# Crossbar transposes for late blocks, relu and last sums on other engines, and a gate in two 16-bit steps, in a fused attention and highway kernel

## Chip, cores and metric

One core of a Trainium2 chip. The metric is device microseconds of one execution; beside it stands one profiled execution, whose span (first to last instruction) is a little shorter than its time. Engines: TensorE (PE), VectorE (DVE), ScalarE (ACT), GpSimd (POOL) and SyncE (SP), which here only issues DMAs.

## What is computed

```python
B, H, S, D = 4, 8, 768, 64        # attention with 4 sink keys and a window of 128
scores = q @ k.T / sqrt(D)
keep   = (key < 4) | ((query - key >= 0) & (query - key < 128))
a      = softmax(where(keep, scores, -1e9))
x      = heads_joined(a @ v)      # 3072 rows x 512
Hm     = maximum(x @ w_h, 0)
T      = sigmoid(x @ w_t + b_t)
out    = T * Hm + (1 - T) * x     # float32
```

## The kernel before

The 3072 rows are 24 blocks of 128, six for each batch. A block needs its own keys and those of the block before it, besides the four sink keys. The first block of a batch has one key chunk, the others two, and from the third on the sinks are added.

For block n: `load_qk` and `load_v` (L86, L87, L94) bring q, k and v in with DMAs that GpSimd issues and that cast to 16 bits. `pe_T` transposes q and k of all heads on TensorE into PSUM, `act_T` (L204) copies them to SBUF as `qk`. `pe_S` makes the scores for two groups of heads, `act_S` (L252) the exponentials `e`, `dve_mask` (L263) masks them. `pe_A` multiplies by v, which carries a column of constants so that the row sums come out as well; `dve_rec` and `dve_x` (L294, L299) normalise to `xh`. `pe_X` and `act_X` (L318) transpose `xh` to `xT`. `pe_Mh` (L341) and `pe_Mt` (L326, L328) are the projections by w_h and w_t; `act_u` (L334) is a tanh. `dve_d` (L347), `dve_e` (L353) and `dve_o` (L359) make the output, and SP stores it (L361).

The column of constants is 2, so that `xh` is x/2, and bias and output are scaled to fit: with u the tanh, `dd` is max(h, 0) - xh, `ee` is (u + 1) times dd, and `otok` is 2 xh + ee. Each of the three is one fused VectorE instruction.

The order on all five queues is written out by hand. In pass i of the main loop stand, among others, `pe_T(i+2)`, the second mask of block i, the scores of i+1, the transpose of x of i-1, the attention sums of i, then the projections of the blocks m whose `m + lag(m)` is i (i-1 here), then the first mask of i+1. The output of a block follows one pass after its projections. A sink product (`pe_sink`, `act_sink`) stands ahead of the projections in two passes of six. `XBAR` names blocks whose x would be transposed by a DMA of SP (`sp_X`); it is empty here. GpSimd's queue holds all the loads, up to eight blocks ahead (`AHEAD`), and a few small steps for the sinks (L213, L130).

PSUM tiles `tp`, `xtp`, `sk`, `hps` and `tps` share a pool of two buffers, `sps` has two of its own, `av` one. SBUF tiles `u`, `dd` and `ee` have three each, `otok` four, `qk` five, `xh` and `xT` seven.

Of the kernel before, what the change touches and what calls it, by code (L numbers as in the profile page):

```python
# [8 lines left out]
FP16 = mybir.dt.float16  # L9
FP32 = mybir.dt.float32  # L10
AF = mybir.ActivationFunctionType
ALU = mybir.AluOpType
# [8 lines left out]
def kernel(  # L21
# [18 lines left out]
    nc = tc.nc  # L40
    P = 128

    B, H, S, D = q.shape
# [5 lines left out]
    NT, DM = out.shape  # L49
# [4 lines left out]
    NB = NT // P  # L54
    NHP = H // 2
# [4 lines left out]

    const = ctx.enter_context(tc.tile_pool(name="const", bufs=1))
    sd_pool = ctx.enter_context(tc.tile_pool(name="p_sd", bufs=AHEAD))
    qkT_pool = ctx.enter_context(tc.tile_pool(name="p_qkT", bufs=5))
    e_pool = ctx.enter_context(tc.tile_pool(name="p_e", bufs=5))
    r_pool = ctx.enter_context(tc.tile_pool(name="p_r", bufs=3))
    x_pool = ctx.enter_context(tc.tile_pool(name="p_x", bufs=7))
    td_pool = ctx.enter_context(tc.tile_pool(name="p_td", bufs=3))
# [5 lines left out]
    NV = AHEAD + 4  # L73
    NS4 = H * NSINK
    KW = NHP * P + 32
    XBAR = ()
    LATE = 0
    v_ring = [const.tile([P, VW], FP16, tag=f"v{i}", name=f"v{i}") for i in range(NV)]
    qk_sd = {}
# [14 lines left out]
        nc.gpsimd.dma_start(out=vt[:, :, 0:D], in_=v[b, :, rows, :].transpose([1, 0, 2]))  # L94

    def init_v(vt):
        nc.vector.memset(vt[:, 0:H * 65].rearrange("p (h e) -> p h e", e=65)[:, :, D:D + 1], 2.0)
        nc.vector.memset(vt[:, H * 65:VW], 0.0)

    warm = const.tile([P, DM], FP16, tag="warm")  # L100
# [5 lines left out]
    bm = const.tile([P, H], FP16, tag="bm", name="bm")  # L106
    wh_sb = const.tile([P, NOC, DM], FP16, tag="wh")
    wt_sb = const.tile([P, NOC, DM], FP16, tag="wt")
    bt32 = const.tile([1, DM], FP32, tag="bt32")
    bt16 = const.tile([P, DM], FP16, tag="bt16")  # L110
# [26 lines left out]
    with tc.manual_schedule(engines={ENG.Pool}):  # L137
        load_qk(0)
        nc.gpsimd.affine_select(
            out=ident, in_=ident, compare_op=ALU.is_equal, fill=0.0,  # L140
# [4 lines left out]
            out=mask[:, 1, :], in_=mask[:, 1, :], compare_op=ALU.is_ge, fill=0.0,  # L145
            base=0, pattern=[[1, P]], channel_multiplier=-1)
        nc.gpsimd.affine_select(
            out=mask[:, 0, :], in_=mask[:, 0, :], compare_op=ALU.is_ge, fill=0.0,
# [6 lines left out]
            out=bm, in_=bm, compare_op=ALU.is_ge, fill=0.0,  # L155
# [10 lines left out]
    def more_constants():  # L166
        nc.vector.memset(bt16, 0.0)
        nc.vector.memset(ones_row, 0.0)
        nc.vector.memset(ones_row[0:1, :], 1.0)
        for i in range(2):  # L170
            nc.vector.memset(ks_bd[i], 0.0)
            nc.vector.memset(vs_bd[i], 0.0)
            nc.vector.memset(es_t[i], 0.0)
        nc.vector.tensor_copy(out=mask0, in_=mask[:, 1, :])
        nc.vector.memset(mask0[0:NSINK, :], 1.0)
        nc.vector.tensor_copy(out=mask1, in_=mask)
        nc.vector.memset(mask1[0:NSINK, 0, :], 1.0)
        nc.vector.tensor_scalar_mul(bt16[0:1, :], bt32, 0.5)

    def sink_ones():  # L180
        for i in range(2):
            nc.vector.tensor_scalar_mul(vs_bd[i][0:NS4, :, D:D + 1],
                                        bm[0:NS4, :].unsqueeze(2), 2.0)

    def warm_up(n):
        w = m_ps.tile([P, DM], FP32, tag="m", name="wps")
# [1 line left out]
            nc.tensor.matmul(w, lhsT=warm[:, 0:P], rhs=warm, start=True, stop=True)  # L188

    qkT, tp_of, s_of, e_of, av_of, rec_of = {}, {}, {}, {}, {}, {}  # L190
    xtp_of, xh_of, xT_of, t_of, u_of, h_of, dd_of, ee_of, sk_of = {}, {}, {}, {}, {}, {}, {}, {}, {}

    def pe_T(n):
        qsd, ksd = qk_sd.pop(n)
# [7 lines left out]
    def act_T(n):  # L202
        qk = qkT_pool.tile([P, 2 * NHP, P], FP16, tag="qk", name="qk")
        nc.scalar.copy(out=qk, in_=tp_of.pop(n))  # L204
        qkT[n] = (qk[:, 0:NHP, :], qk[:, NHP:2 * NHP, :])

    def pool_sink(b):
# [123 lines left out]

    def act_u(n):
        u = td_pool.tile([P, DM], FP16, tag="u", name="u")
        nc.scalar.activation(out=u, in_=t_of.pop(n), func=AF.Tanh)  # L334
        u_of[n] = u

    def pe_Mh(n):
        xT = xT_of[n]
        hps = m_ps.tile([P, DM], FP32, tag="m", name="hps")
        for kc in range(NOC):  # L340
            nc.tensor.matmul(hps, lhsT=xT[:, kc, :], rhs=wh_sb[:, kc, :],  # L341
                             start=(kc == 0), stop=(kc == NOC - 1))
        h_of[n] = hps

    def dve_d(n):
        dd = td_pool.tile([P, DM], FP16, tag="dd", name="dd")
        nc.vector.scalar_tensor_tensor(out=dd, in0=h_of.pop(n), scalar=0.0, in1=xh_of[n],  # L347
                                       op0=ALU.max, op1=ALU.subtract)
        dd_of[n] = dd

    def dve_e(n):
        ee = td_pool.tile([P, DM], FP16, tag="ee", name="ee")
        nc.vector.scalar_tensor_tensor(out=ee, in0=u_of.pop(n), scalar=1.0, in1=dd_of.pop(n),  # L353
                                       op0=ALU.add, op1=ALU.mult)
        ee_of[n] = ee

    def dve_o(n):
        otok = o_pool.tile([P, DM], FP32, tag="otok", name="otok")
        nc.vector.scalar_tensor_tensor(out=otok, in0=xh_of.pop(n), scalar=2.0, in1=ee_of.pop(n),  # L359
                                       op0=ALU.mult, op1=ALU.add)  # L360
        nc.sync.dma_start(out=out[n * P:(n + 1) * P, :], in_=otok)  # L361

    def on(n):
        return 0 <= n < NB
# [14 lines left out]
    with tc.manual_schedule(engines={ENG.PE, ENG.DVE, ENG.Activation, ENG.SP, ENG.Pool}):  # L379
        for i in range(-2, NB + 2):  # L380
            ms = [m for m in range(2, NB) if m + lag(m) == i]
            os_ = [m for m in range(1, NB) if m + lag(m) == i - 1]
            if i == -2:
                warm_up(8)
                more_constants()
                pe_T(0)
                act_T(0)
            elif i == -1:
                pe_S(0, 0)
                act_S(0, 0)  # L390
                pe_S(0, 1)
                act_S(0, 1)
                dve_mask(0, 0)
                dve_mask(0, 1)
                pe_T(1)
                act_T(1)
                pe_A(0)
                dve_rec(0)
                dve_x(0)
                pe_S(1, 0)  # L400
                act_S(1, 0)
                pe_S(1, 1)
                act_S(1, 1)
                dve_mask(1, 0)
                dve_mask(1, 1)
                pe_X(0)
                act_X(0)
                spare(3)
                pe_A(1)
                dve_rec(1)  # L410
                dve_x(1)
                sink_ones()
                sink_v(0, nc.vector)
            elif i == 0:
                pe_Mt(0)
                act_u(0)
                pe_X(1)
                act_X(1)
                pe_Mt(1)
                pe_Mh(0)  # L420
                dve_d(0)
                act_u(1)
                pe_T(2)
                act_T(2)
                dve_e(0)
                pe_Mh(1)
                dve_o(0)
                dve_d(1)
            elif i == 1:
                pe_S(2, 0)  # L430
                act_S(2, 0)
                dve_mask(2, 0)
                pe_S(2, 1)
                pe_T(3)
                act_T(3)
                act_S(2, 1)
                pe_sink(2)
                act_sink(2)
            else:
                if on(i + 2):  # L440
                    pe_T(i + 2)
                    act_T(i + 2)
                if on(i):
                    dve_mask(i, 1)
                for o in os_:
                    dve_e(o)
                if on(i + 1):
                    pe_S(i + 1, 0)
                    pe_S(i + 1, 1)
                if on(i - 1) and i - 1 not in XBAR and i - 1 > 1:  # L450
                    pe_X(i - 1)
                    act_X(i - 1)
                if on(i + 1):
                    act_S(i + 1, 0)
                for o in os_:
                    dve_o(o)
                if on(i):
                    pe_A(i)
                    dve_rec(i)
                    dve_x(i)  # L460
                    if i in XBAR:
                        sp_X(i)
                if has_sink(i + 1):
                    pe_sink(i + 1)
                    act_sink(i + 1)
                if on(i + 1):
                    act_S(i + 1, 1)
                for m in ms:
                    pe_Mh(m)
                    dve_d(m)  # L470
                    pe_Mt(m)
                    act_u(m)
                if on(i + 1):
                    dve_mask(i + 1, 0)
            if on(i + 2) and (i + 2) % NSC == 0:
                b = (i + 2) // NSC
                pool_sink(b)
                if b:
                    sink_v(b, nc.gpsimd)
                if b + 1 < B:  # L480
                    load_sink_v(b + 1)
            for n in {-2: range(3, AHEAD + 1), 0: [], 1: [10, 11]}.get(i, [i + 2 + AHEAD]):
                if n < NB:
                    if n > 3:
                        load_qk(n)
                    load_v(n)
# [35 lines left out]
```

## Time and profile before

| | |
|---|---|
| time, median of 2 | 129.54 us (129.47 to 129.61) |
| span of the profiled execution | 127.8 us |
| PE busy, matmul | 110.1 us (86%) |
| DVE busy | 101.8 us (80%) |
| ACT busy | 97.6 us (76%) |
| POOL busy | 74.9 us (59%), nearly all before 78 us |
| mean granted TensorE clock | 0.992 |
| 16 DMA engines | 90% or more till about 80 us, then about 20% |

Busy time of one engine is not its distance from its peak, and shares over the whole span mix the start, the passes and the end. The chain that ended last is read back from the last instruction, each step to what released it; its pieces in order of time show which dependence sets the length of a pass. Timelines of single engines list instructions with their starts, so that the distance from one start to the next can be read, which is what adds up on an engine whose neighbours overlap a little.

### The profile page before, as it was taken

The numbers are of one execution on the slowest core, as the hardware profiler recorded it, in microseconds if no ns is written. First come the engines' busy times: TensorE is split into PE (matmuls) and PEld (weight loads), VectorE is DVE, ScalarE is ACT, GpSimd is POOL, SyncE is SP. The second block draws the span as 40 slices with busy tenths as digits, with TensorE's granted clock in tenths as the row PEclk, the third lists the DMA queues.
The fourth block names the chain that finished last, engine by engine and source line by source line (L and its number), as shares of the span: only waits on it lengthen the run. The fifth ranks groups of instructions, "written<-read, shape, count | busy, mean of one in ns | idle before, by whom it ended". The sixth has DMA issues, their size and how long they took to land.

```text
span 127.8 us, 3253 instructions
## 1 busy us (share of the span) xinstructions
PE 110.1 (86%) x1315; PEld 67.9 (53%) x1315; DVE 101.8 (80%) x214; ACT 97.6 (76%) x129; POOL 74.9 (59%) x98
## 2 busy tenths in 40 slices
PE   6758989569999899999998999999989999999620
PEld 2236434447755574586555656755655666564300
DVE  6544626495999898998998998989989999899760
ACT  4066435999897998998987989989969989893310
POOL 6999939999899989999999995005000000000000
PEclk9999999999999999999999999999999999999996
DMA  0999999999999999999999999922022202210222
GB/s 1 105 126 140 165 153 157 180 181 197 160 156 204 204 180 201 163 199 200 164 199 194 208 159 205 186 95 82 8 82 82 82 5 82 82 60 28 82 82 82
DMA packets 79728, 17.00 MB, mean 133 GB/s; under 512 B 75617, under 2 KB 76641, under 8 KB 79714
## 3 DMA queue, kind: packets, MB, share of 16 engines
q0 software_dynamic: 76256, 10.51, 122.6%
q1 hardware_dynamic: 3458, 6.30, 13.3%
q8 instruction: 10, 0.16, 0.5%
q14 instruction: 4, 0.03, 0.1%
HBM read 21.01 MB, written 6.29 MB: 214 GB/s over the span
## 4 chain that ended last, share of the span: by engine, by line
PE 39%; ACT 29%; DMA 12%; POOL 9%; DVE 6%; issue 3%; POOLq 0%; ACTq 0%
PE tps L328 14%; PE hps L341 11%; ACT qk L204 10%; DMA wh_sb<-in_moe_w_h_dram 7%; ACT u L334 6%; ACT e L252 6%; ACT xT L318 5%; DMA ksd<-in_k_dram 5%; PE tps L326 4%; POOL qsd L86 3%; PE sps L244 3%; PE av L280 2%; POOL ksd L87 2%; POOL v L94 2%; PE xtp L313 2%
## 5 line engine op out<-in xcount | busy, mean ns | idle before, releaser
L252 ACT ACTIVATE e<-sps,ebias 128x1024 f16<-128x1024 f32 (+1 forms) x48 | 48.6, 1054 | 1.8 <-PE sps L244 1.8
L263 DVE TENSOR_TENSOR e<-e,mask 128x1024 f16<-128x1024 f16 (+1 forms) x48 | 29.1, 640 | 4.7 <-ACT e L252 4.6
L204 ACT COPY qk<-tp 128x1024 f16<-128x1024 f16 x24 | 24.2, 1009 | 6.4 <-PE tp L199 6.4
L341 PE MATMUL hps<-wh_sb,xT 128*128 128x512 f16 x96 | 24.8, 380 | 3.4 <-ACT xT L318 2.9
L334 ACT ACTIVATE u<-tps 128x512 f16<-128x512 f32 x24 | 14.3, 597 | 16.0 <-PE tps L328 16.0
L328 PE MATMUL tps<-wt_sb,xT 128*128 128x512 f16 x96 | 25.0, 384 | 0.1
L86 POOL DMA_DIRECT2D qsd<-in_q_dram x24 | 22.4, 932 | 3.4 <-DMA wh_sb<-in_moe_w_h_dram 2.0
L94 POOL DMA_DIRECT2D v<-in_v_dram x24 | 22.3, 929 | 0.5 <-DVE dd L347 0.3
L347 DVE SCALAR_TENSOR_TENSOR dd<-hps,xh 128x512 f16<-128x512 f32 x24 | 16.6, 691 | 7.4 <-PE hps L341 5.7
L87 POOL DMA_DIRECT2D ksd<-in_k_dram x24 | 22.1, 920 | 0.5 <-PE tps L328 0.3
L353 DVE SCALAR_TENSOR_TENSOR ee<-u,dd 128x512 f16<-128x512 f16 x24 | 16.5, 689 | 3.5 <-ACT u L334 3.2
L280 PE MATMUL av<-v,e 128*128 128x66 f16 x352 | 17.7, 197 | 0.6 <-DVE e L263 0.5
L328 PEld LDWEIGHTS <-xT 128*128 128x128 f16 x96 | 9.4, 98 | 15.0 <-issue 4.1
L299 DVE TENSOR_TENSOR xh<-av,rec 128x512 f16<-128x512 f32 x24 | 16.6, 692 | 0.8
L359 DVE SCALAR_TENSOR_TENSOR otok<-xh,ee 128x512 f32<-128x512 f16 x24 | 16.6, 692 | 0.8
L280 PEld LDWEIGHTS <-e 128*128 128x128 f16 x352 | 15.2, 100 | 2.2 <-DVE e L263 1.9
L244 PE MATMUL sps<-qk 64*128 64x128 f16 x352 | 14.6, 223 | 1.5 <-ACT qk L204 1.5
L318 ACT COPY xT<-xtp 128x512 f16<-128x512 f16 x24 | 14.4, 598 | 0.4 <-PE xtp L313 0.3
L341 PEld LDWEIGHTS <-xT 128*128 128x128 f16 x96 | 7.9, 97 | 12.0 <-ACT xT L318 5.7
L244 PEld LDWEIGHTS <-qk 64*128 64x128 f16 x352 | 10.4, 97 | 4.8 <-ACT qk L204 1.4
L199 PE MATMUL tp<-ident,ksd 128*128 128x128 f16 x96 | 9.8, 227 | 1.7 <-DMA ksd<-in_k_dram 1.6
L197 PEld LDWEIGHTS <-qsd 128*128 128x128 f16 x96 | 7.2, 100 | 6.8 <-DMA qsd<-in_q_dram 2.2
(51 smaller groups left out, 100.2 us busy)
## 6 DMA issues: line engine op xcount, KB each, us to landing
out_dram<-otok SPq DMA_DIRECT2D x24, 256.0 KB, 4.5
qsd<-in_q_dram POOLq DMA_DIRECT2D x24, 128.0 KB, 6.5
ksd<-in_k_dram POOLq DMA_DIRECT2D x24, 128.0 KB, 6.5
v<-in_v_dram POOLq DMA_DIRECT2D x24, 128.0 KB, 6.7
wt_sb<-in_moe_w_t_dram POOLq DMA_DIRECT2D x1, 512.0 KB, 7.3
wh_sb<-in_moe_w_h_dram POOLq DMA_DIRECT2D x1, 512.0 KB, 9.4
vd<-in_v_dram POOLq DMA_DIRECT2D x4, 4.0 KB, 4.9
bt<-in_moe_b_t_dram SPq DMA_DIRECT2D x1, 2.0 KB
```

The lines of the kernel that those rows point to most:

```text
L86: nc.gpsimd.dma_start(out=qsd, in_=q[b, :, rows, :].transpose([1, 0, 2]))
L87: nc.gpsimd.dma_start(out=ksd, in_=k[b, :, rows, :].transpose([1, 0, 2]))
L94: nc.gpsimd.dma_start(out=vt[:, :, 0:D], in_=v[b, :, rows, :].transpose([1, 0, 2]))
L204: nc.scalar.copy(out=qk, in_=tp_of.pop(n))
L244: nc.tensor.matmul(sps[:, hh, o:o + P], lhsT=kk[rows, hp, :], rhs=qT[rows, hp, :], start=True, stop=True)
L252: nc.scalar.activation(out=e.rearrange("p a b c d -> p a (b c d)"), in_=sps[:, :, 0:2 * np_ * P], func=AF.Exp, bias=ebias, scale=SCALE)
L263: nc.vector.tensor_tensor(out=ev, in0=ev, in1=m.unsqueeze(1).to_broadcast([P, 4, np_ * P]), op=ALU.mult)
L280: nc.tensor.matmul(av[:, g, 2 * hl + hh, 0:_AVN], lhsT=e[:, hh, hl, pc, :], rhs=vt[:, 65 * h:65 * h + _AVN], start=first, stop=False, skip ...
L318: nc.scalar.copy(out=xT, in_=xtp_of.pop(n))
L328: nc.tensor.matmul(tps, lhsT=xT[:, kc, :], rhs=wt_sb[:, kc, :], start=False, stop=(kc == NOC - 1))
L334: nc.scalar.activation(out=u, in_=t_of.pop(n), func=AF.Tanh)
L341: nc.tensor.matmul(hps, lhsT=xT[:, kc, :], rhs=wh_sb[:, kc, :], start=(kc == 0), stop=(kc == NOC - 1))
```

## The change

- q and k of blocks 12 to 23 are no longer transposed on TensorE and copied by ScalarE. `sp_T` issues two transposing DMAs from SP instead, four passes ahead of the block (in pass i for block i+4); `qk` gets eight buffers.
- x of blocks 15 to 21 is transposed by a DMA of SP (`XBAR`), and the projections of those blocks come two passes behind, not one.
- For blocks 14 to 22 (`LT`) ScalarE makes relu(h) in 16 bits (`act_r`), `dd` is a difference of two 16-bit tiles in SBUF, and the last sum runs on GpSimd.
- The column of constants becomes 1, so that `xh` is x. The gate is one step (0.5 u + 0.5, tile `tg`) and `ee` a product of two 16-bit tiles; the last sum needs no factor.

On SP the transposes stand between the output stores, in the order of the program. In pass i that is: q and k of i+4, the store of the block whose output is due, x of i. On GpSimd the sums of blocks 14 to 22 stand behind the loads of the last block. In pass 16 no projection is due, and in pass 23 there are two, of 21 and 22.

```diff
-    qkT_pool = ctx.enter_context(tc.tile_pool(name="p_qkT", bufs=5))
+    qkT_pool = ctx.enter_context(tc.tile_pool(name="p_qkT", bufs=8))
...
-    XBAR = ()
+    XBAR = range(15, 22)
+    XT = range(12, NB)
+    LT = range(14, NB - 1)
...
-        nc.vector.memset(... [:, :, D:D + 1], 2.0)
+        nc.vector.memset(... [:, :, D:D + 1], 1.0)
...
+    def sp_T(n):
+        qsd, ksd = qk_sd.pop(n)
+        qk = qkT_pool.tile([P, 2 * NHP, P], FP16, tag="qk", name="qk")
+        nc.sync.dma_start_transpose(out=qk[:, 0:NHP, :], in_=qsd.rearrange("p h d -> p (h d)"))
+        nc.sync.dma_start_transpose(out=qk[:, NHP:2 * NHP, :],
+                                    in_=ksd.rearrange("p h d -> p (h d)"))
+        qkT[n] = (qk[:, 0:NHP, :], qk[:, NHP:2 * NHP, :])
...
-        nc.scalar.activation(out=u, in_=t_of.pop(n), func=AF.Tanh)
+        nc.scalar.activation(out=u, in_=t_of.pop(n), func=AF.Tanh, scale=0.5)
...
+    def act_r(n):
+        rl = td_pool.tile([P, DM], FP16, tag="rl", name="rl")
+        nc.scalar.activation(out=rl, in_=h_of.pop(n), func=AF.Relu)
+        rl_of[n] = rl
...
     def dve_d(n):
+        if n in LT:
+            nc.vector.tensor_tensor(out=dd, in0=rl_of.pop(n), in1=xh_of[n], op=ALU.subtract)
+        else:
+            nc.vector.scalar_tensor_tensor(out=dd, in0=h_of.pop(n), scalar=0.0, in1=xh_of[n],
+                                           op0=ALU.max, op1=ALU.subtract)
...
     def dve_e(n):
-        nc.vector.scalar_tensor_tensor(out=ee, in0=u_of.pop(n), scalar=1.0, in1=dd_of.pop(n),
-                                       op0=ALU.add, op1=ALU.mult)
+        tg = td_pool.tile([P, DM], FP16, tag="tg", name="tg")
+        nc.vector.tensor_scalar(out=tg, in0=u, scalar1=0.5, scalar2=0.5, op0=ALU.mult, op1=ALU.add)
+        nc.vector.tensor_tensor(out=ee, in0=tg, in1=dd_of.pop(n), op=ALU.mult)
...
     def dve_o(n):
-        nc.vector.scalar_tensor_tensor(out=otok, in0=xh_of.pop(n), scalar=2.0, in1=ee_of.pop(n),
-                                       op0=ALU.mult, op1=ALU.add)
+        eng = nc.gpsimd if n in LT else nc.vector
+        eng.tensor_tensor(out=otok, in0=xh_of.pop(n), in1=ee_of.pop(n), op=ALU.add)
...
-                if on(i + 2):
+                if on(i + 4) and i + 4 in XT:
+                    sp_T(i + 4)
+                if on(i + 2) and i + 2 not in XT:
                     pe_T(i + 2)
                     act_T(i + 2)
...
                 for m in ms:
                     pe_Mh(m)
+                    if m in LT:
+                        act_r(m)
                     dve_d(m)
```

More of the change, by code (lines that the diff above doesn't have):

```diff
@@ L96, in init_v @@
     def init_v(vt):
-        nc.vector.memset(vt[:, 0:H * 65].rearrange("p (h e) -> p h e", e=65)[:, :, D:D + 1], 2.0)
+        nc.vector.memset(vt[:, 0:H * 65].rearrange("p (h e) -> p h e", e=65)[:, :, D:D + 1], 1.0)
         nc.vector.memset(vt[:, H * 65:VW], 0.0)
@@ L177, in more_constants @@
         nc.vector.memset(mask1[0:NSINK, 0, :], 1.0)
-        nc.vector.tensor_scalar_mul(bt16[0:1, :], bt32, 0.5)
+        nc.vector.tensor_copy(out=bt16[0:1, :], in_=bt32)
     def sink_ones():
@@ L182, in sink_ones @@
             nc.vector.tensor_scalar_mul(vs_bd[i][0:NS4, :, D:D + 1],
-                                        bm[0:NS4, :].unsqueeze(2), 2.0)
+                                        bm[0:NS4, :].unsqueeze(2), 1.0)
     def warm_up(n):
@@ L190 @@
     qkT, tp_of, s_of, e_of, av_of, rec_of = {}, {}, {}, {}, {}, {}
-    xtp_of, xh_of, xT_of, t_of, u_of, h_of, dd_of, ee_of, sk_of = {}, {}, {}, {}, {}, {}, {}, {}, {}
+    xtp_of, xh_of, xT_of, t_of, u_of, h_of, dd_of, ee_of, sk_of, rl_of = {}, {}, {}, {}, {}, {}, {}, {}, {}, {}
     def pe_T(n):
@@ L343, in pe_Mh @@
         h_of[n] = hps
+    def act_r(n):
+        rl = td_pool.tile([P, DM], FP16, tag="rl", name="rl")
+        nc.scalar.activation(out=rl, in_=h_of.pop(n), func=AF.Relu)
+        rl_of[n] = rl
     def dve_d(n):
         dd = td_pool.tile([P, DM], FP16, tag="dd", name="dd")
-        nc.vector.scalar_tensor_tensor(out=dd, in0=h_of.pop(n), scalar=0.0, in1=xh_of[n],
-                                       op0=ALU.max, op1=ALU.subtract)
+        if n in LT:
[3 more added lines that the diff above has]
+                                           op0=ALU.max, op1=ALU.subtract)
         dd_of[n] = dd
     def dve_e(n):
+        u = u_of.pop(n)
+        tg = td_pool.tile([P, DM], FP16, tag="tg", name="tg")
+        nc.vector.tensor_scalar(out=tg, in0=u, scalar1=0.5, scalar2=0.5, op0=ALU.mult, op1=ALU.add)
         ee = td_pool.tile([P, DM], FP16, tag="ee", name="ee")
-        nc.vector.scalar_tensor_tensor(out=ee, in0=u_of.pop(n), scalar=1.0, in1=dd_of.pop(n),
-                                       op0=ALU.add, op1=ALU.mult)
+        nc.vector.tensor_tensor(out=ee, in0=tg, in1=dd_of.pop(n), op=ALU.mult)
         ee_of[n] = ee
```

## The prediction

> **What bounds the kernel now.** I read the page first, then the chain that ended last, then the timelines of single engines. The page shows three engines loaded alike, so shares decide nothing. What does is the chain; here is one pass of the loop in it (start us, us, work):
>
> ```profile
> 87.57 1.04 PE hps L341 x4
> 88.61 0.22 PE tps L326
> 88.82 0.88 PE tps L328 x4
> 89.72 0.60 ACT u L334
> 90.32 0.90 ACT qk L204
> 91.22 0.50 ACT xT L318
> 91.77 1.04 PE hps L341 x4
> ```
>
> The pass goes from TensorE to ScalarE and back: two projections, tanh, the copy of q/k for a later block, the copy of x, next projection: 4.20 us. Passes with a sink step take 4.4 to 4.6; starts of hps in TensorE's timeline at 52.59, 78.70 and 104.81 give 26.11 us for six blocks, 4.35 each. VectorE is just under that. Its own pace shows near the end, where it waits for nothing (timeline of VectorE):
>
> ```profile
> 112.27 0.69 DVE L353 SCALAR_TENSOR_TENSOR ee<-u,dd 128x512 f16<-128x512 f16 x1
> 112.99 0.69 DVE L359 SCALAR_TENSOR_TENSOR otok<-xh,ee 128x512 f32<-128x512 f16 x1
> 113.60 0.20 DVE L294 RECIPROCAL rec<-av 128x8 f32<-128x8 f32 x1
> 113.84 0.69 DVE L299 TENSOR_TENSOR xh<-av,rec 128x512 f16<-128x512 f32 x1
> 114.44 0.68 DVE L347 SCALAR_TENSOR_TENSOR dd<-hps,xh 128x512 f16<-128x512 f32 x1
> 115.04 1.28 DVE L263 TENSOR_TENSOR e<-e,mask 128x1024 f16<-128x1024 f16 x2
> 116.24 0.69 DVE L353 SCALAR_TENSOR_TENSOR ee<-u,dd 128x512 f16<-128x512 f16 x1
> ```
>
> From ee to ee: 3.97 us. The starts are what to add up (neighbours overlap by 0.08): ee 0.72, otok 0.61, rec 0.24, xh 0.60, dd 0.60, two masks 1.20. So taking copies off ScalarE alone would uncover VectorE after 0.4 us a block.
>
> **The change, by stretches.** Marks are the starts of hps of block m: 57.04 for m=8, 83.15 for m=14, 87.57 for m=15, 120.21 for m=23. The profiled execution's span is 127.8 us, the median time 129.54, so 1.7 lies around the span; savings in the span are taken off the median.
>
> *Up to m=8* nothing on the path goes: q/k of blocks up to 11 still take TensorE and ScalarE. Till 28.6 the loads rule. VectorE changes only ee (below), covered by the 4.35 pass. Cost 0; if the new gate step is held up by GpSimd, up to 0.1 a pass for eight passes, 0.8.
>
> *The gate.* One 0.69 us instruction becomes tg, a 16-bit tensor-scalar, and a 16-bit product. The product has the shape of the mask on a first chunk (two 128x512 in 0.75): 0.375, and 0.03 for the handoff. For tg the trace has no 128x512 row. Low end: a 128x256 16-bit copy took 0.150, four columns a cycle would add 0.07: 0.22. High end: a tensor-scalar of 8 columns (L182) took up to 0.611 beside GpSimd's descriptor work. I take 0.22 and a mean hold-up of 0.13 while GpSimd still issues loads (to about 78 us), since the 0.150 copy also ran beside such an issue. Pass of VectorE: 3.97 - 0.72 + 0.26 + 0.41 = 3.92, or 4.05 held up. Output sums keep a 32-bit result, so L359's 0.69 stays where VectorE does them; the ones column and the scales cost nothing anew.
>
> *m=8 to m=14, six passes, 26.11 now.* q/k of blocks 12 on no longer use TensorE (0.54 of its 4.00 a pass, by starts) nor ScalarE (0.90). Ring without them: 4.20 - 0.90 = 3.3; TensorE 3.46, with a sink step 3.91. VectorE now sets it: 6 x 4.05 - 0.53 (block 12's mask is half as wide) = 23.8. Gain 2.3; ends 3.1 (tg 0.22) and 0.8 (tg 0.61).
>
> *m=14 on.* relu goes to ScalarE (L334's shape: 0.60), dd becomes 16-bit (0.30 by starts), the sum leaves VectorE: its pass falls to 0.56 + 0.24 + 0.60 + 0.30 + 1.20 = 2.9. ScalarE: e 2.1, relu 0.5, u 0.5, es 0.36 in a sink pass: 3.1 to 3.5. TensorE 3.2 to 3.7. But a new ring closes: relu, dd, masks, attention sums, hps, relu. From the end of the masks (116.32) to the end of the hps behind them (117.78) is 1.46, so: 0.60 + 0.03 + 0.30 + 1.28 + 1.46 + 0.03 = 3.70, and 0.45 more when the sink product lies ahead of hps. That is what late blocks run at, not 2.9.
>
> The blocks 15 to 21 also come one pass later (lag 2 against 1). From m=14 to m=15 there are then two passes: hps 1.04, relu 0.66 with handoffs, dd 0.30, masks 1.20, gate 0.56, rec and xh 0.84, masks 1.28, to hps 0.43: 6.3 against 4.42. Then six passes to m=21: 6 x 3.70 + 2 x 0.45 - 0.7 (first chunk, block 18) = 22.4. Then hps and tps of 21 and 22 run back to back (2 x 1.96), transpose of x 23 and, behind tanh 22, its copy: 5.2 to m=23. Sum 33.9 against 120.21 - 83.15 = 37.1: gain 3.2. The end from m=23 on loses 0.05 (tg and product against ee).
>
> *Work moved to queues.* SP gets two transposes a pass from pass 8 on (blocks 12 to 23) and one of x in passes 15 to 21, between the output stores, in order. Each waits for its load; q(12) is issued at 40.4 and lands some 7 us later, its transpose is due in SP after the store of pass 7, about 48, and its score product comes three passes, 12 us, later. x has nearly two passes, 7 us. So one transpose's delay is hidden; their total is not. Price by these rows (queue; packets, MB, share of 16 engines):
>
> ```profile
> q0 software_dynamic: 76256, 10.51, 122.6%
> q1 hardware_dynamic: 3458, 6.30, 13.3%
> ```
>
> A 256 KB store took 13.3% x 127.8 / 24 = 0.71 us of all engines, so 128 KB in large pieces 0.35. A load of 1024 small pieces took 122.6% x 127.8 x 1024 / 76256 = 2.1. Transposes start from SP like the stores but cut rows small: I take 1.0. Three a pass in passes 15 to 19 then need 3.0 of about 3.6. Behind a slow one stand the stores, so otok's four buffers, and the next x.
>
> The Trainium skill, DMA: Bandwidth & Descriptors, Latency and other measured facts, gives a transpose 261 GB/s, by which one would be 0.5 us, an estimate; no row here shows one.
>
> GpSimd gets nine sums. Its nearest row is the sink product (32x512): 1.03, but 1.48 once:
>
> ```profile
> 47.35 0.69 DVE L359 SCALAR_TENSOR_TENSOR otok<-xh,ee 128x512 f32<-128x512 f16 x1
> 47.46 1.48 POOL L130 TENSOR_TENSOR vs<-vd,bm 32x512 f16<-32x512 f16 x1
> ...
> 6.63 0.26 DVE L174 COPY mask<-mask 128x128 f16<-128x128 f16 x1 [1.71 <-POOL mask L144]
> 7.07 0.15 DVE L176 COPY mask<-mask 128x256 f16<-128x256 f16 x1
> 6.52 0.32 POOL L147 TENSOR_SCALAR_AFFINE_SELECT mask<-mask 128x128 f16<-128x128 f16 x1
> ```
>
> The 1.48 began under a VectorE instruction with two SBUF inputs, and 0.45 passed until its normal 1.03 could end; the 128-column copy took longer than a 256-column one and ended with GpSimd's select. So the two exclude each other. In the new loop a sum starts when ee ends, 0.67 after the masks; VectorE then does rec and xh, which read PSUM, and dd is due 2.1 after the masks. A sum of 1.03 to 1.4 fits in between: cost 0. No load is left behind it on GpSimd; late sums hold stores, not the path. ee waits for a sum three blocks back, long done.
>
> The Trainium skill, SBUF — State Buffer, Who interferes with whom, speaks against the change: the shared port pair is locked for a whole instruction, with the loser fully blocked. By it a sum that reached into dd or the masks would cost its whole remainder; the two rows above agree with it, and as the sums lie in this order the total by it stays 124.0.
>
> Sum: 2.3 + 3.2 + 0.05 = 5.5; 129.5 - 5.5 = **124.0 us**. Ends: 0.8 + 3.2 - 0.8 gives 126.3; 3.1 + 3.2 and handoffs of the new ring shorter by 0.1 in nine passes give 122.3, and 0.1 a pass less on VectorE early, 121.7.
>
> **Rivals.**
> - *Transposes become the bound* (slower side). Place: SP's queue in passes 15 to 19, 15 transposes in 4.0 + 2.6 + 3 x 3.8 = 18 us. Slack of x 7.4 less 2.0 landing: 5.4. Free up to 23.5 / 15 = 1.57 us each; the gain of 5.5 is gone at 1.93, where slower begins; at 2.1, the load's price, 15 x 2.1 - 23.5 = 8 late: 132; at 2.5, 14 late: 138. For: 16 engines stay 90% busy till 80 us, stores land in 5.3 there. Against: after 84 they are 20% busy and a store lands in 2.0.
> - *GpSimd's sum holds VectorE*: should it take twice its row, 2.1 or more, it ends 0.7 into the time of dd: 0.7 x 7 passes, 5 lost: 129. Decides from 1.4 us. For: 128 partitions and 32-bit results against 32 and 16-bit. Against: the row's 1.03 has as many columns.
> - *tg held up to 0.6 throughout the load phase*: 124.0 + 1.5 + 0.8 = 126.3, and with holds in the late ring 0.1 to 0.2 a pass: 127.5.
> - *The lag eats it*: if x is late from latency alone once, 1 to 2 us: 125.5, inside the forecast.
>
> **How the numbers follow.** This kernel's measurement can tell about 2% from no change: 126.95 to 132.1 counts as same. Forecast, with the lag case, 0.66 (121.7 to 126.5); tg held 0.14, half of it under 126.95; transposes bound 0.15, a third of it under 132.1; GpSimd's sum 0.05, same. Faster 0.66 + 0.07 = 0.73, same 0.07 + 0.05 + 0.05 = 0.17, slower 0.10. The range 121.5 to 130 leaves out 0.12 of the transposes' case and some 0.06 below.
>
> **What would show it.** Right: hps starts about 4.0 apart between m=8 and m=14 with VectorE without gaps; 3.7 and 4.15 after; m=14 near 80.9, m=23 near 114.7; q/k copies on ScalarE ending with block 11; sums on GpSimd of 1.0 to 1.4 ending before dd; TensorE never waiting for a DMA after 50 us. Wrong: TensorE waiting for qk or xT from a transpose; 4.3 apart with gaps ahead of ee; dd or masks lengthened beside GpSimd. A time above 127 means one of these.

## The result and the profile after

The changed kernel takes 143.62 us (median of 2 runs, 143.32 to 143.92) against 129.54: a ratio of 1.110, 95% interval 1.102 to 1.119. It is slower by 11%, where 124.0 was forecast. The profiled execution has a span of 142.2 us against 127.8, and a mean granted clock of 0.918 against 0.992. Some executions of one kernel take over 1.5% longer than its fastest, and the ratios here leave them out.

The page of the changed kernel: total busy time of engines, the clock and the DMA engines in 40 slices (3.56 us each), DMA queues (packets, MB, share of 16 engines), median time from issue to landing. The share adds up the time of every packet, also where packets overlap, and so goes past 100%.

```profile
span 142.2 us, 3101 instructions
PE 110.0 (77%) x1191; PEld 62.2 (44%) x1191; DVE 94.4 (66%) x229; ACT 89.1 (63%) x119; POOL 84.2 (59%) x107
...
PEclk9999999999999999999995599985685799999996
DMA  1999999999999999999999999999999792311132
...
q0 software_dynamic: 76256, 10.51, 117.7%
q1 hardware_dynamic: 20322, 10.36, 37.6%
...
qk<-qsd SPq DMA_TRANSPOSE x12, 7.8
```

The same row of the DMA engines before, in slices of 3.20 us:

```profile
DMA  0999999999999999999999999922022202210222
```

VectorE and ScalarE lost 7.4 and 8.5 us of work, as the change means, and the span grew by 14.4. What grew is the stretch in which the DMA engines are full: before, the nines end at about 83 us, now between 110 and 117. The clock digits show two dips, at 75 to 82 us and from 92 to 114 us.

The chain that ended last, from the middle of the kernel on:

```profile
75.92 1.03 PE sk L232 x8
76.96 1.71 PE hps L351 x4
...
88.91 9.34 DMA xT<-xh
98.30 1.90 PE hps L351 x4
100.42 7.17 DMA xT<-xh
107.63 1.89 PE hps L351 x4
```

Before, the chain went from TensorE to ScalarE and back. Now its two longest pieces here are transposes of x in flight, 9.34 and 7.17 us, with TensorE idle, and the projection behind each takes 1.9 us instead of 1.04. The starts of `hps` give the ledger:

| stretch | before | after | after less before |
|---|---|---|---|
| m=8 starts at | 57.04 | 57.22 | +0.2 |
| m=8 to 11 | 12.82 | 11.21 | -1.6 |
| m=11 to 14 | 13.29 | 18.21 | +4.9 |
| m=14 to 17 | 12.82 | 26.66 | +13.8 |
| m=17 to 23 | 24.24 | 21.61 | -2.6 |
| m=23 starts at | 120.21 | 134.91 | +14.7 |

Up to m=11 the engines' part of the change brings 1.6 us; then two stretches lose 18.7. A part of that is the schedule: m=15 comes two passes after m=14, and 21 and 22 come back to back, so the stretch from 14 to 17 holds a pass that the one from 17 to 23 gives back. Run 11 below has the same lag with every x on time; there its two passes, m=15 to 16, take 6.05 us against 4.20 before. So about 1.9 us of the 13.8 are lag, and the 2.6 is not all a gain of the engines.

**The first loss, 75 us.** GpSimd's timeline (start, duration, and in brackets the idle time before with what ended it):

```profile
68.20 0.88 POOL L89 DMA_DIRECT2D ksd<-in_k_dram  x1 [2.94 <-PE av L290]
70.26 0.87 POOL L96 DMA_DIRECT2D v<-in_v_dram  x1 [1.18 <-DMA qsd<-in_q_dram]
...
74.55 0.87 POOL L96 DMA_DIRECT2D v<-in_v_dram  x1
75.42 0.45 POOL L223 COPY ks<-qk 64x16 f16<-64x16 f16 x2
...
97.90 0.87 POOL L96 DMA_DIRECT2D v<-in_v_dram  x1 [1.24 <-DMA qsd<-in_q_dram]
98.79 1.16 POOL L380 TENSOR_TENSOR otok<-xh,ee 128x512 f32<-128x512 f16 x1
```

Between its loads GpSimd now waits, mostly for earlier loads to land (`<-DMA`); before, it issued these back to back:

```profile
64.26 1.03 POOL L94 DMA_DIRECT2D v<-in_v_dram  x1
65.13 0.91 POOL L213 COPY ks<-qk 64x16 f16<-64x16 f16 x2
...
77.29 0.98 POOL L94 DMA_DIRECT2D v<-in_v_dram  x1
```

Loads now land late, so its in-order queue is late, and the small sink copy L223 (L213 before) behind them starts at 75.42. TensorE waits 3.6 us for it ahead of `sk`, and `hps` stands behind `sk`. The last two lines of GpSimd's timeline show the second effect: v of block 23, the last load, is issued at 97.90. Before it was at 77.29.

**The second loss, 88 to 113 us.** SP's queue in the changed kernel:

```profile
88.91 1.23 SPq L316 DMA_TRANSPOSE xT<-xh  x1
90.53 1.26 SPq L212 DMA_TRANSPOSE qk<-qsd  x1
91.89 3.68 SPq L213 DMA_TRANSPOSE qk<-ksd  x1
99.98 0.34 SPq L381 DMA_DIRECT2D out_dram<-otok  x1
100.42 1.24 SPq L316 DMA_TRANSPOSE xT<-xh  x1
```

The transpose for block 15 goes out at 88.91 and lands 9.3 us later, among the loads. The one for block 16 could have gone out at 92.30, when VectorE finishes `xh` (91.61 + 0.69). It goes out at 100.42. Until 95.57 SP is held by the transpose of k ahead of it (3.68 us, where most take 1.2; why this one is long is not shown). Then the store of block 14 stands ahead, which waits for block 14's sum on GpSimd (98.79), which waits for the last load (97.90). So 3.3 of the 8.1 us are SP's own, and 4.8 come from GpSimd. One late load queue reaches TensorE by way of GpSimd, a store and SP.

Where do the loads lose their time? The DMA queues between 57 and 77 us (packets, MB, share of 16 engines) and the landing time of v, first before, then after:

```profile
q0 software_dynamic: 20831, 2.62, 206.7%
q1 hardware_dynamic: 588, 1.07, 14.8%
...
v<-in_v_dram POOLq DMA_DIRECT2D x7, 128.0 KB, 6.5
```

```profile
q0 software_dynamic: 12156, 1.53, 121.0%
q1 hardware_dynamic: 4691, 2.04, 58.9%
...
v<-in_v_dram POOLq DMA_DIRECT2D x4, 128.0 KB, 14.3
```

In both kernels the DMA engines are full in this stretch (the rows above). In the second the transposes (queue 1) take room, and 8675 load packets fewer get through in 20 us. Loads issued there took 6.2 to 6.5 us to land before; in the changed kernel they take 14.3 to 14.7.

### The profile page after: what moved, and what is told of

It is laid out like the page before. It is cut to its first block, busy times and chain, and to the rows that moved or that the text cites. A ratio compares the mean times of both kernels' runs of the same rounds, so it can differ in the third digit from the quotient of the medians.

```text
span 142.2 us, 3101 instructions
## 1 busy us (share of the span) xinstructions
PE 110.0 (77%) x1191; PEld 62.2 (44%) x1191; DVE 94.4 (66%) x229; ACT 89.1 (63%) x119; POOL 84.2 (59%) x107
## 4 chain that ended last, share of the span: by engine, by line
DMA 39%; PE 27%; ACT 10%; POOL 9%; DVE 9%; issue 3%; POOLq 0%; DVEq 0%; ACTq 0%
DMA xT<-xh 12%; PE hps L351 11%; DMA v<-in_v_dram 10%; DMA wh_sb<-in_moe_w_h_dram 7%; PE tps L338 6%; DMA qsd<-in_q_dram 6%; DMA ksd<-in_k_dram 4%; DVE e L273 4%; ACT e L262 3%; PE av L290 3%; POOL qsd L88 2%; ACT rl L357 2%; PE sps L254 2%; POOL ksd L89 2%; POOL v L96 2%
## 5 line engine op out<-in xcount | busy, mean ns | idle before, releaser
L351 PE MATMUL hps<-wh_sb,xT 128*128 128x512 f16 x96 | 27.3, 411 | 11.0 <-DMA xT<-xh 8.8
L338 PE MATMUL tps<-wt_sb,xT 128*128 128x512 f16 x96 | 27.4, 412 | 0.1
L380 POOL TENSOR_TENSOR otok<-xh,ee 128x512 f32<-128x512 f16 x9 | 10.4, 1153 | 26.6 <-DVE ee L374 24.3
L344 ACT ACTIVATE u<-tps 128x512 f16<-128x512 f32 x24 | 14.3, 596 | 17.4 <-PE tps L338 17.4
L351 PEld LDWEIGHTS <-xT 128*128 128x128 f16 x96 | 8.7, 102 | 20.0 <-DMA xT<-xh 9.1
L363 DVE TENSOR_TENSOR dd<-rl,xh 128x512 f16<-128x512 f16 x9 | 4.3, 475 | 18.9 <-ACT rl L357 18.9
L338 PEld LDWEIGHTS <-xT 128*128 128x128 f16 x96 | 10.0, 105 | 15.3 <-issue 5.5
L206 ACT COPY qk<-tp 128x1024 f16<-128x1024 f16 x12 | 12.1, 1009 | 6.9 <-PE tp L201 6.9
L365 DVE SCALAR_TENSOR_TENSOR dd<-hps,xh 128x512 f16<-128x512 f32 x15 | 10.3, 689 | 8.6 <-PE hps L351 8.3
L357 ACT ACTIVATE rl<-hps 128x512 f16<-128x512 f32 x9 | 5.3, 588 | 15.1 <-PE hps L351 15.1
L374 DVE TENSOR_TENSOR ee<-tg,dd 128x512 f16<-128x512 f16 x24 | 11.0, 457 | 1.3
L328 ACT COPY xT<-xtp 128x512 f16<-128x512 f16 x17 | 10.0, 591 | 1.8 <-PE xtp L323 1.7
```

Of the source, the lines that this page charges most:

```text
L338: nc.tensor.matmul(tps, lhsT=xT[:, kc, :], rhs=wt_sb[:, kc, :], start=False, stop=(kc == NOC - 1))
L344: nc.scalar.activation(out=u, in_=t_of.pop(n), func=AF.Tanh, scale=0.5)
```

## The experiments

The theory that the profile suggests: the 16 DMA engines are shared and full until the loads are done, a transpose takes its time out of the loads, and the in-order queues of GpSimd and SP carry the delay to TensorE. Rivals: the data dependence on transposes; the order on GpSimd or SP alone; relu's place; the sums holding VectorE. Ratios are to the kernel before, with 95% intervals.

**1 to 3: parts of the change.** First without the transposes of q and k:

```diff
-    XT = range(12, NB)
+    XT = ()
```

> The changed kernel with q and k of all blocks back on TensorE and ScalarE; the seven transposes of x stay with SP. Theory 'shared engines': the 24 transposes of q and k take time of the 16 DMA engines from the loads, so without them the loads run as before (landing 6 to 7 us, last one about 84 us), the x transposes, which start at 80 us, land in 3 to 6 us, no hps waits for xT, and the time is 127 to 131 us. Rival 'late results' (a transpose is simply long, and what comes out of SP's queue comes too late): the waits of hps for xT, 8.8 us in the changed kernel, stay, and the time is 136 us or more. Rival 'engines' (relu, gate or GpSimd's sums cost it): 140 us or more.

Measured: 130.78 us, 1.007 (1.003 to 1.010). The seven transposes of x land in 2.5 us (median), no projection waits for one, and the last load goes out at 77.73. The transposes of q and k are the only difference, so it is they that make x late in the changed kernel.

Then the other half, q and k by DMA and no transposes of x:

```diff
-    XBAR = range(15, 22)
+    XBAR = ()
```

> The changed kernel with x of all blocks transposed on TensorE; q and k of blocks 12 on stay with SP. 'Shared engines': loads still land in 12 us and more, the sink copies on GpSimd still come late, only the 8.8 us of waits for xT go and in part come back as waits for loads or sinks: 132 to 138 us. 'Late results': without x there is no late result left, 125 to 128 us. 'Engines': 140 us or more.

Measured: 140.18 us, 1.081 (1.074 to 1.088), worse than foreseen. Most of the loss needs no transpose of x. Why it is more than was foreseen shows in its VectorE timeline, and then in GpSimd's beside it:

```profile
97.22 2.13 DVE L374 TENSOR_TENSOR ee<-tg,dd 128x512 f16<-128x512 f16 x1
...
100.27 2.99 DVE L363 TENSOR_TENSOR dd<-rl,xh 128x512 f16<-128x512 f16 x1
```

```profile
97.00 0.88 POOL L96 DMA_DIRECT2D v<-in_v_dram  x1 [0.86 <-DVE e L273]
97.89 1.16 POOL L380 TENSOR_TENSOR otok<-xh,ee 128x512 f32<-128x512 f16 x1
...
99.73 1.03 POOL L132 TENSOR_TENSOR vs<-vd,bm 32x512 f16<-32x512 f16 x1
100.73 2.25 POOL L380 TENSOR_TENSOR otok<-xh,ee 128x512 f32<-128x512 f16 x2
```

The sums, held up behind late loads, come out together and at the wrong moment: `ee` and `dd`, 0.42 to 0.43 us each elsewhere in this run, take 2.13 and 2.99. `ee` starts while GpSimd issues the last load and ends at 99.35, 0.30 after a sum; `dd` starts under a sink product and ends at 103.26, 0.28 after the next two sums. Both have two operands in SBUF, as the sum has. From m=17 at 97.79 the next projection then needs 11.0 us, of which `sk` spends 2.85 waiting for a transposed q.

Third, neither:

```diff
-    XBAR = range(15, 22)
-    XT = range(12, NB)
+    XBAR = ()
+    XT = ()
```

> The changed kernel without any transpose on SP; relu on ScalarE, sums on GpSimd and the new gate stay. 'Shared engines' and 'late results' both: loads as before, no stalls, 126 to 130 us (ScalarE has relu and the copies of q, k and x: 2.1 + 0.5 + 0.5 + 0.9 + 0.5 = 4.5 us a pass from block 14 on, so little or no gain). 'Engines': 140 us or more.

Measured: 132.94 us, 1.026 (1.021 to 1.031): slower than before, not faster. The change loses something without a single transpose. ScalarE's timeline of one late pass:

```profile
95.17 1.01 ACT L206 COPY qk<-tp 128x1024 f16<-128x1024 f16 x1
96.08 0.59 ACT L328 COPY xT<-xtp 128x512 f16<-128x512 f16 x1
96.56 2.13 ACT L262 ACTIVATE e<-sps,ebias 128x1024 f16<-128x1024 f32 x2
98.56 0.62 ACT L357 ACTIVATE rl<-hps 128x512 f16<-128x512 f32 x1
...
99.87 1.01 ACT L206 COPY qk<-tp 128x1024 f16<-128x1024 f16 x1 [0.21 <-PE tp L201]
```

From copy to copy 4.70 us with 0.2 idle: with relu and both copies ScalarE is the bound. Whether relu on ScalarE pays where the copies have gone, no run shows by itself.

**4: transposes that nobody waits for.** The kernel before, with the changed kernel's 31 transposes at its places in SP's queue, but from a constant tile into scratch:

```diff
+    def sp_idle(n):
+        for _ in range(n):
+            sc = idle_pool.tile([P, NHP, P], FP16, tag="sc", name="sc")
+            nc.sync.dma_start_transpose(out=sc, in_=warm)
...
+                if i + 4 in IDLE_QK:      # range(12, NB)
+                    sp_idle(2)
...
+                    if i in IDLE_X:       # range(15, 22)
+                        sp_idle(1)
```

> The kernel before, with 31 transposes added on SP at the places of the changed kernel, 128x512 of 16 bits from a constant tile into scratch that nobody reads: they wait for nothing and nothing waits for them. 'Shared engines': they displace the loads all the same; at some 1.2 to 1.4 us of all 16 engines each, 31 of them make 37 to 43 us of DMA work more, the loads end near 115 us and not 84, and the time is 135 to 145 us. 'Late results' and 'engines': 129.5 us, since no result is used.

Measured: 135.13 us in the profiled run, as the theory of shared engines has it, and 139.26 in the other. Both are above every run of the kernel before (129.26 to 130.40), but they lie too far apart for a ratio. No data depend on these transposes, no instruction of another engine was changed, and the profiled span is 5.6 us longer. Its TensorE timeline, and its DMA queues from 57 to 77 us:

```profile
77.68 0.97 PE L230 MATMUL sk<-qk,ks 128*128 128x128 f16 x8 [4.00 <-POOL ks L221]
78.44 1.91 PE L349 MATMUL hps<-wh_sb,xT 128*128 128x512 f16 x4
```

```profile
q0 software_dynamic: 9664, 1.22, 106.4%
q1 hardware_dynamic: 5336, 2.43, 64.1%
```

The same wait for the same sink copy as in the changed kernel, the same shift in the queues, and the last load at 97.49 instead of 77.29. 21 transposes are issued before it: 20.2 / 21 = 0.96 us each. In the changed kernel 19 stand before it: 20.6 / 19 = 1.08. These are averages, and a little of each may not be the DMA engines' (some loads wait for late TensorE work, `<-PE av` above). That the transposes push the loads back is shown here; it does not depend on what they carry.

**5: GpSimd's order.** The sink's small steps go to VectorE, out of the load queue:

```diff
-            nc.gpsimd.tensor_copy(out=dst[:, :, NSINK * hh:NSINK * hh + NSINK],
+            nc.vector.tensor_copy(out=dst[:, :, NSINK * hh:NSINK * hh + NSINK],
...
-                    sink_v(b, nc.gpsimd)
+                    sink_v(b, nc.vector)
```

> The changed kernel with the sink copies (L223) and the sink products of v (L132) on VectorE, not in GpSimd's queue behind the loads. Theory 'order': the DMA engines are slowed, but what stops the passes is the sink copy that stands behind loads eight blocks ahead; then the 3.6 us wait at 72 to 76 us goes and the passes to m=14 keep 3.7 to 4.0 us: 143.6 falls to 134 to 138 us. Theory 'engines': the DMA engines have too much to do until about 113 us whatever the order; the wait comes back at another place (a transposed q/k, x or v that is late) and the time stays at 140 to 145 us.

Measured: 141.68 us, 1.097 (1.094 to 1.101). The first stall is gone: m=12, 13 and 14 start at 75.06, 78.76 and 83.64. The second stays: `hps` of 15 and 16 wait 4.36 and 4.21 us for x, and start at 96.34 and 106.09. The place of the sink steps on GpSimd is worth 2 us of the 14; the loads' delay stays. The sums still stand behind the late loads in this run; what their place is worth was not run.

**6: the gate alone.**

```diff
-    XBAR = range(15, 22)
-    XT = range(12, NB)
-    LT = range(14, NB - 1)
+    XBAR = ()
+    XT = ()
+    LT = ()
```

> The kernel before with the gate step and the 16-bit product alone: no transpose on SP, relu and sums on VectorE as before. If the extra of the kernel without transposes over before (132.9 against 129.6) comes from relu on ScalarE: 129.0 to 130.0 us here. If it comes from the gate step, which takes a lock that GpSimd's descriptor work also needs: 131 to 133 us.

Measured: 129.75 us, 1.003 (1.001 to 1.006). `tg` takes 0.294 us (median; longest 0.793), `ee` 0.426. The gate costs nothing that matters and gains nothing; that TensorE and ScalarE set the pass, as in the chain before, is the likely reason.

**7: idle transposes after the loads.** Again the kernel before, with 32 idle transposes, now four in each of eight passes from pass 16 on:

```diff
+    IDLE_QK = range(20, 28)      # three at each pass's start
+    IDLE_X = range(16, 24)       # one where x would be
```

> The kernel before with 32 unused transposes, four a pass, from pass 16 on (about 85 us), when the loads have landed. 'Shared engines': nothing is left to displace but the stores, so 129 to 130.5 us, against 137.2 with as many spread from pass 8 on. If a transpose costs the compute engines something itself (SBUF, ports, SP's queue): 132 us or more.

Measured: 140.0 us, 1.083 (1.079 to 1.088), a plain miss. The computation was not touched: `hps` of 23 starts at 120.76 (before 120.21). The time is at the end, in SP's timeline:

```profile
121.01 5.14 SPq L213 DMA_TRANSPOSE sc<-warm  x4
126.25 0.52 SPq L369 DMA_DIRECT2D out_dram<-otok  x1
```

Four transposes hold SP 5.14 us, 1.29 each, and with a store that is more than a pass of 4.3. The stores fall behind and the last one goes out at about 134, nine us after its data are ready. The DMA engines are idle enough (they land in 2.4 us, median); the issuing queue is not. So there are two prices: about 1.0 us of the DMA engines, which matters while they are full, and 1.2 to 1.3 us of SP's queue, which adds up in any stretch.

**8: the changed kernel with later transposes.** q and k from block 18 only, which are issued from pass 14 on; relu back on VectorE:

```diff
-    XT = range(12, NB)
+    XT = range(18, NB)
...
-        if n in LT:
-            nc.vector.tensor_tensor(out=dd, in0=rl_of.pop(n), in1=xh_of[n], op=ALU.subtract)
-        else:
-            nc.vector.scalar_tensor_tensor(out=dd, in0=h_of.pop(n), scalar=0.0, in1=xh_of[n],
-                                           op0=ALU.max, op1=ALU.subtract)
+        nc.vector.scalar_tensor_tensor(out=dd, in0=h_of.pop(n), scalar=0.0, in1=xh_of[n],
+                                       op0=ALU.max, op1=ALU.subtract)
...
-                    if m in LT:
-                        act_r(m)
```

> The changed kernel with two things mended: q and k go to SP only from block 18 on (issued from pass 14, when the loads are nearly done), and relu stays in VectorE's instruction on PSUM; the sums of blocks 14 to 22 stay on GpSimd, x of 15 to 21 on SP. 'Shared engines': no stall, late passes 3.4 to 3.9 us, hps of block 23 at about 115 us and the time 124 to 127 us, faster than before. If late transposes stall the passes all the same: 129 us or more.

Measured: not as fast as foreseen, 129.12 us, the median of ten runs scattered from 126.84 to 132.12 (the kernel before: 129.50, 128.96 to 130.72). The ratio, 0.982 (0.976 to 0.989), is that of the three fastest. What sets those apart is not shown; the trace is of a run of 129.13. Its TensorE timeline shows what remains:

```profile
91.58 1.04 PE L351 MATMUL hps<-wh_sb,xT 128*128 128x512 f16 x4 [1.47 <-DMA xT<-xh]
...
107.91 1.04 PE L351 MATMUL hps<-wh_sb,xT 128*128 128x512 f16 x4 [2.02 <-DMA xT<-xh]
```

Three transposes and a store in a pass, with x last in the queue and due first: the loss of 14 us is gone, but x still comes late twice.

**9 to 12: which parts are worth keeping.** The next four all have the gate, and relu back on VectorE as in 8. Run 9 adds only the sums on GpSimd:

```diff
-    XBAR = range(15, 22)
-    XT = range(12, NB)
+    XBAR = ()
+    XT = ()
```

> The kernel before with the new gate and with the sums of blocks 14 to 22 on GpSimd; relu stays in VectorE's instruction on PSUM, no transpose on SP. If relu on ScalarE is what costs the 3 us of the kernel without transposes (132.9): the passes keep ScalarE's ring of 4.2 us and the time is 129 to 130 us. If GpSimd's sums hold VectorE: 132 to 133 us.

Measured: 129.58 us, 0.999 (0.996 to 1.002). The sums, each 1.15 us, neither cost nor gain. Against run 3 this puts relu on ScalarE at 132.94 - 129.58 = 3.4 us, without transposes.

Run 10 adds q and k of blocks 18 to 23 by DMA:

```diff
-    XBAR = range(15, 22)
-    XT = range(12, NB)
+    XBAR = ()
+    XT = range(18, NB)
```

> As the run before, and q and k of blocks 18 to 23 transposed by SP, issued from pass 14 on (about 79 us), when the loads are nearly done; x stays on TensorE. 'Shared engines': nothing is displaced and a tile is due three passes after its transpose starts, so from pass 16 on the ring loses the 0.9 us copy and runs at 3.5 to 3.9 us, seven passes gain 0.5 to 0.7 each: 124.5 to 126.5 us. If a transpose behind the loads stalls the passes however far ahead it is issued: 129 us or more.

Measured: 126.51 us, 0.976 (0.972 to 0.980), the upper edge of what was foreseen: faster than both kernels, and the best here. q and k land in 3.2 and 4.9 us (medians) and nobody waits for them; late projections start 3.3 to 4.1 us apart.

Run 11 has x of blocks 16 to 21 by DMA instead:

```diff
-    XBAR = range(15, 22)
-    XT = range(12, NB)
+    XBAR = range(16, 22)
+    XT = ()
```

> As the gate and sums alone, and only x of blocks 16 to 21 transposed by SP, from about 88 us on, after the loads. 'Shared engines': they land in 2.5 to 3 us, no wait of hps for xT; ScalarE keeps the 0.9 us copy of q and k, a pass takes 3.8 to 4.1 us, the later projections cost about 1 us at the seams: 127 to 129 us. If the lag of one more pass is what costs: 130 us or more.

Measured: 126.96 us, 0.981 (0.976 to 0.987), just under what was foreseen; x lands in 2.4 us (median). Either set of transposes gains alone. Both together, run 8, show no more than that even in the three fastest runs.

Run 12 is run 10 with the sums back on VectorE:

```diff
-    LT = range(14, NB - 1)
+    LT = ()
```

> The late transposes of q and k with all sums on VectorE. VectorE's pass is then 3.9 us by its rows; if it sets the late passes: 127 to 128.5 us, some 2 us above the same with the sums on GpSimd. If ScalarE's and TensorE's ring sets them: no difference to it.

Measured: 127.87 us, 0.988 (0.982 to 0.994), as foreseen. Its VectorE now sets the pass, with hardly a gap from one pair of masks to the next:

```profile
97.41 1.28 DVE L273 TENSOR_TENSOR e<-e,mask 128x1024 f16<-128x1024 f16 x2
...
101.44 1.28 DVE L273 TENSOR_TENSOR e<-e,mask 128x1024 f16<-128x1024 f16 x2
```

That is 4.03 us. The sums on GpSimd, worth nothing in run 9, are worth 127.87 - 126.51 = 1.4 us once ScalarE's copies are gone: parts of a change have their value only together with what else is short.

## Why the prediction was wrong

**The step that failed is "Work moved to queues".** It took 1.0 us of the DMA engines for a transpose, and that came out (0.96 and 1.08 by the averages above). It said that "one transpose's delay is hidden; their total is not", and then it added the total up only for passes 15 to 19, against SP's slack. It should have been added up from pass 8 on, against the DMA engines, whose row of nines stood in the page until 83 us. 19 transposes at 1.0 us ahead of the last load, issued at 77.3, put that load at 96 to 97; it was at 97.9. The price was there, and so was the full resource; the sum over the right stretch was not made. I had read the full engines as latency, 7 us for one transfer, and not as a queue that has no room. That 1.0 came out was in part luck. It was picked between 0.35 and 2.1, and the 2.1 for a load was a misreading: shares of packets that overlap were taken for time of the engines. From 57 to 77 us 20831 load packets, about 20 loads, went through beside the stores, so a load needs at most 1.0 us. The lower estimate that the prediction gives beside its own was half of what the runs show.

**"Late sums hold stores, not the path" failed with it.** "No load is left behind it on GpSimd" is true, but the loads stand before the sums, and behind the stores on SP stands the next x. Naming what is queued behind a waiting instruction needs both queues: sum behind load, store behind sum, transpose behind store.

**The rival "transposes become the bound" had the kind and not the place.** It put the trouble in SP in passes 15 to 19, at a price of 1.93 us or more. At a price of 1.0 it happened in the DMA engines from pass 8 on. Its remark for it, "16 engines stay 90% busy till 80 us", was the case, and the answer against it, that they are 20% busy after 84, held only as long as the loads were not pushed back. SP's own time of 1.2 to 1.3 us for a transpose was in no sum. In run 7 it decides alone; here it adds to the wait of x.

The other steps:

- *Up to m=8*, cost 0: 57.22 against 57.04. Right.
- *The gate.* `tg` 0.22 with a hold-up of 0.13: measured 0.29 (median in run 6); product 0.375: 0.425. The costs hold within 0.1, and run 6 shows no loss. The rival of a `tg` held up throughout did not come.
- *m=8 to 14*, 23.8: the first three passes went in 11.21 against a rate of 4.05 x 3 = 12.2, better than forecast, as one pass takes 3.66. Then the wait for the sink copy took all of it.
- *The ring from m=14 on*, 3.70 a pass and 4.15 with a sink product. Late VectorE timeline of the changed kernel, two passes:

```profile
115.47 0.43 DVE L363 TENSOR_TENSOR dd<-rl,xh 128x512 f16<-128x512 f16 x1 [1.48 <-ACT rl L357]
115.81 1.29 DVE L273 TENSOR_TENSOR e<-e,mask 128x1024 f16<-128x1024 f16 x2
...
119.22 0.42 DVE L363 TENSOR_TENSOR dd<-rl,xh 128x512 f16<-128x512 f16 x1 [0.55 <-ACT rl L357]
...
123.89 0.43 DVE L363 TENSOR_TENSOR dd<-rl,xh 128x512 f16<-128x512 f16 x1 [1.47 <-ACT rl L357]
```

  From dd to dd 3.75 and then 4.67; the next, to 127.64, is 3.75 again. The ring is the one described, VectorE waits for relu in each of these passes, and 3.70 was right. The sink pass was mis-sized by 0.5: not only does the sink product precede `hps` (0.45), the small exponential and the second `e` also stand ahead of relu on ScalarE (relu starts at 114.87, when `e` from 113.87 ends, though `hps` ended at 114.33). `dd` in 16 bits costs 0.34 by starts, not 0.30.
- *The lag*, 6.3 from m=14 to 15: 11.7, the late x. The stretch as laid out can't be seen in this run; its end, 5.2 from m=21 to 23, took 5.21.
- *GpSimd's sum*, 1.03 to 1.4: 1.15, and run 9 shows it free. That it excludes VectorE's two-input instructions was right, and that the order keeps them apart was right too, as long as the sums are not late. In run 2 they were, and the cost foreseen for that came.
- *The end* from m=23 on: 0.05 foreseen; span less start of `hps` 23 is 7.3 us, before 7.6.

One thing was missing altogether: the clock. Each stall of about 4 us in the changed kernel is followed by a projection of 1.9 us instead of 1.04 and by slower work for some us more; the granted clock over 86.6 to 113.3 us is 0.74 on average. TensorE: Matmul & The Clock Gate in the Trainium skill (Part 1: The HAM clock gate) says that TensorE drops to half rate after an idle window of about 3.4 us. Most rows agree: stalls of 3.6 to 4.6 us were followed by projections of 1.89 to 1.91 us, the shorter ones of 1.47 and 2.02 in run 8 by 1.04. Run 2 differs: a stall of 3.20 at 76.00 was followed by 1.91, and so was one of 2.85 at 108.42 that came soon after another of 2.85, at 103.92. By these runs the edge lies below 3.2 us, and two shorter stalls close together can do the same.

That the gains were real, and what they were worth, runs 10 and 11 show: 2.4% and 1.9%, when the transposes start after most loads are issued, and only one kind of them. What stays open is how run 8 would do with x ahead of q and k in SP's queue, and how much of the second loss each part of its chain (x in flight, the k transpose that held SP, the store behind the late sum) costs by itself; neither was run.

## What to carry to other kernels

Before moving work onto DMA, add the moved transfers' time to the DMA engines over exactly the stretch in which they will be issued; where that row is full, each transfer delays everything behind it, and the last load moves by the sum. Then follow every in-order queue one step further than the instruction that waits (load, sum, store, transpose here), because a "harmless" late store may stand in front of the one transfer that the bound engine needs. And test parts in pairs: relu on ScalarE cost 3.4 us without the transposes, and the sums on GpSimd were worth nothing alone and 1.4 us beside them.

## What the runs showed of the hardware

- A DMA transpose of a 128x512 16-bit tile mostly holds SP's queue 1.19 to 1.37 us (3.68 once in the changed kernel), where a 256 KB store mostly holds it 0.33 to 0.53. It lands in 2.4 to 2.5 us (medians of runs 1, 7 and 11) on quiet engines; in the changed kernel the median of q is 7.8 us, and one x took 9.3 among the loads.
- On average one pushes the stream of loads back by 0.96 to 1.08 us (run 4 and the changed kernel), 1.4 to 1.5 times what the 256 KB store was estimated to take of all engines before (0.71), though it moves half the bytes.
- A VectorE instruction with two SBUF operands that meets GpSimd's sums ends only after them: in run 2 one of 0.43 us took 2.13 beside a load's issue and one sum, another 2.99 beside a sink product and two sums.
- TensorE runs at about half speed after a stall of 3.2 to 4.6 us, and not after one of 2.02: the next four 512-column matmuls took 1.89 to 1.91 us instead of 1.04.
